# First weight of the first FFN: its loads, conversion and first plain tile, two steps sooner

## The chip, the cores and the metric

One core of a Trainium2 chip runs the whole program. The metric is the device time of one execution in microseconds (us); the median of several executions is compared. PE is TensorE (matmul), DVE is VectorE, ACT is ScalarE, POOL is GpSimd, SP is the engine whose queue issues most of the DMAs here.

## What is computed

A decayed linear attention (retention) over 4 batches, 8 heads, 768 positions and a head size of 64, followed by two feed-forward layers on the 3072 x 512 result.

```python
for t in range(S):
    state = gamma[None, :, None, None] * state + np.einsum('bhd,bhe->bhde', k[:, :, t], v[:, :, t])
    y[:, :, t] = scale * np.einsum('bhd,bhde->bhe', q[:, :, t], state)
...
h = x @ w_in                      # 3072x512 @ 512x2048
g = np.maximum(0.01 * h, h)
x = g @ w_out                     # 3072x2048 @ 2048x512
...
h = x @ w_in                      # the second layer, with its own weights
g = h * (1.0 / (1.0 + np.exp(-1.702 * h)))
y = g @ w_out
```

The weights arrive as 64-bit words (low and high 32-bit halves) and the kernel turns them into 32-bit floats itself.

## The kernel before, in words

**Order of the work.** The program is scheduled by hand: each engine, and SP's queue, executes its instructions in the order in which the Python code emits them. So the order of the calls in the loop of `retention()` (lines 378 to 404) is the order on every engine.

**Retention, 24 steps.** A step `s` is one chunk of 128 positions of one batch (4 batches of 6 chunks, `c` is the chunk's number in its batch), all 8 heads. `a_load(s)` (L263) brings 1 MB of q, k and v into a ring of four places. `a_scores(s)` (L269) makes the scores on PE (L277) and multiplies them by the decay mask on DVE (L280); its PSUM banks 0 and 1 are the only ones for scores, so the scores of the next step wait for that mask product. `a_decay(s)` (L283) scales k on ACT in eight instructions (L288), and is left out in the last chunk of a batch (steps 5, 11, 17, 23). `a_out(s)` (L290) has the matmuls for the state (L300), for scores times v (L307) and for state times q (L313), and the state's scaling on DVE (L316); L300 and L316 are missing in the last chunk of a batch, L313 in the first. `a_store(s, o)` (L320) scales the result out of PSUM: in steps 0 to 7 in three DVE instructions (L332), afterwards in one (L345). In steps 0 to 3, which make the tokens of block 0, ACT then rounds the result to the matmul format (L341) and POOL subtracts to get the remainder (the subtraction of `subtract`, L151): these two parts are the operand `x0`, 128 columns of it per step.

**The loop** prepares step `s + 1`'s scores, runs `a_out(s)`, does the first half of a weight's work (`work_first`, L216), `a_store(s)`, the second half (`work_last`, L222), `a_decay(s + 2)`, `a_load(s + 4)` and last the plain tiles of that step (`ffn_in(0, m)`, L231).

**Weight work.** Weight `m` of 16 is one 128 x 512 slice of the first layer's `w_in`. `load_raw(m)` (L165) loads 512 KB through SP into a ring of three places. `convert(m)` (L193) runs two ACT instructions (L172, L173) and four DVE instructions (L176, L178, L180, L182), from a ring of two places. `work_last(n)` rounds weight `n` up (L191: on POOL for weights 0 and 1, on DVE afterwards) and finishes weight `n - 1`: a rounding cast on ACT (L154) and a subtraction on DVE (L151) give the weight's two parts. `work_first(n)` also loads raw weight `n + 2`, before it converts weight `n`.

**Plain tiles.** `ffn_in(0, m)` multiplies weight `m` with block 0 of the tokens: 12 matmuls of 128 x 512 (L238), three for each quarter of the 512 inputs: weight's high part with the remainder of `x0`, high with high, the weight's remainder with the high part. ACT applies the leaky ReLU (L242) and its queue stores the result (L244).

**When.** The constant `W0` and the list `now_in` set the step of each tile, and the condition in line 385 derives from them the steps of the weight work:

```python
W0 = 6
now_in = [[m for m in range(KF) if W0 + m * (N_STEPS - W0) // KF == s] for s in range(N_STEPS)]
...
if s >= W0 - 2 and done[0] < KF + 1 and (s <= W0 or now_in[s - 1]):
```

Before, weight work begins in step 4, tile 0 is in step 6, tiles 0 to 7 are in steps 6 to 13, tiles 8 to 15 in steps 15 to 22. Raw weights 0 and 1 are loaded at the end of steps 1 and 2, raw weight 2 in step 4.

**Afterwards** the blocks 1 to 5 of the first layer's `x @ w_in` follow (L238 again), then three products in a seven-product form (L776, L583, L776).

Of the kernel before, what the change touches and what calls it, by code (L numbers as in the profile page):

```python
# [87 lines left out]
def retention_two_ffn(ctx: ExitStack, tc: tile.TileContext, qkv, consts, small, w1i, w1o, w2i, w2o, scratch, out):  # L88
# [76 lines left out]
    def load_raw(m):  # L165
        raw[m] = t = next(raw_ring).bitcast(U32)
        nc.sync.dma_start(out=t, in_=w1i[m].bitcast(U32).rearrange("p (f two) -> p f two", two=2))
# [39 lines left out]
    def x_split(q, k):  # L207
        split(xs[q % 2][k][:, 0], xs[q % 2][k][:, 1], x_raw[:, k])
        if k == NP - 1 and q + 1 < NB:
            x_load(q + 1)  # L210

    W0 = 6
    now_in = [[m for m in range(KF) if W0 + m * (N_STEPS - W0) // KF == s] for s in range(N_STEPS)]
    done = [0]

    def work_first(n):  # L216
        if n + 2 < KF:
            load_raw(n + 2)
        if n < KF:
            convert(n)  # L220

    def work_last(n):  # L222
        if n < KF:
            round_up(*conv[n], nc.gpsimd if n < 2 else nc.vector)
        if 0 < n <= KF:
            finish(n - 1)
# [4 lines left out]
    def ffn_in(blk, m, place=None):  # L231
        h = banks[:, h_banks[i_h[0] % len(h_banks)]]
        i_h[0] += 1
        w = wt[m].rearrange("p s (k f) -> p s k f", k=NP)
        i = 0
        for k in range(NP):
            for a, c in ((0, 1), (0, 0), (1, 0)):
                nc.tensor.matmul(out=h, lhsT=w[:, a, k], rhs=xs[blk % 2][k][:, c], start=(i == 0),  # L238
                                 stop=(i == 3 * NP - 1), skip_group_check=True)
                i += 1  # L240
        t = next(g_ring) if place is None else place
        nc.scalar.activation(out=t, in_=h, func=AF.Lrelu)  # L242
        if place is None:
            nc.scalar.dma_start(out=gd1[m][:, blk * TB : blk * TB + TB], in_=t)  # L244

    def retention():
# [16 lines left out]
        def a_load(s):  # L263
            ins[s] = next(in_ring)
            n = 2 if s < 3 else 4
            for i in range(0, 4, n):
                nc.sync.dma_start(out=ins[s][:, i : i + n], in_=qkv[s, :, i : i + n])

        def a_scores(s):  # L269
            t = ins[s]  # L270
            qT = t[:, 0].rearrange("p (n i) -> p n i", n=NP)
            kT = t[:, 1].rearrange("p (n i) -> p n i", n=NP)
            ps = banks[:, 0:2].rearrange("p e (n i) -> p e n i", n=NP)
            for n in range(NP):
                for e in range(2):
                    r = slice(D * e, D * e + D)
                    nc.tensor.matmul(out=ps[:, e, n], lhsT=kT[r, n], rhs=qT[r, n], start=True, stop=True,  # L277
                                     skip_group_check=True)
            sm = next(sm_ring)
            nc.vector.tensor_tensor(out=sm, in0=ps, in1=mask, op=ALU.mult)  # L280
            sc_t[s] = sm

        def a_decay(s):  # L283
            b, c = steps[s]
            if c < NC - 1:
                ks_t[s] = ins[s][:, 2].rearrange("p (h d) -> p h d", h=H)
                for h in range(H):
                    nc.scalar.activation(out=ks_t[s][:, h], in_=ks_t[s][:, h], func=AF.Copy, scale=kdec[:, c, h : h + 1])  # L288

        def a_out(s):  # L290
            b, c = steps[s]
            t = ins.pop(s)
            sm, ks = sc_t.pop(s), ks_t.pop(s, None)
            q = t[:, 0].rearrange("p (n i) -> p n i", n=NP)
            v = t[:, 3].rearrange("p (n f) -> p n f", n=NP)
            if c < NC - 1:
                for n in range(NP):
                    for e in range(2):
                        r = slice(D * e, D * e + D)
                        nc.tensor.matmul(out=kv[r, n], lhsT=ks[:, 2 * n + e], rhs=v[:, n, r],  # L300
                                         start=(c == 0 and n == 0), stop=True, skip_group_check=True)
            o = next(o_ring)
            out = lambda n, e: o[D * (e ^ (n & 1)) : D * (e ^ (n & 1)) + D, n % 2, n // 2 * P : n // 2 * P + P]
            for n in range(NP):
                for e in range(2):
                    r = slice(D * e, D * e + D)
                    nc.tensor.matmul(out=out(n, e), lhsT=v[:, n, r], rhs=sm[:, e, n], start=(n < 2),  # L307
                                     stop=(c == 0), skip_group_check=True)
            if c > 0:
                for n in range(NP):  # L310
                    for e in range(2):
                        r = slice(D * e, D * e + D)
                        nc.tensor.matmul(out=out(n, e), lhsT=st[c % 2][r, n], rhs=q[r, n], start=False, stop=True,  # L313
                                         skip_group_check=True)
            if c < NC - 1:
                nc.vector.tensor_tensor(out=st[(c + 1) % 2], in0=kv, op=ALU.mult,  # L316
                                        in1=gdec[:, c + 1, :].unsqueeze(2).to_broadcast([P, NP, D]))
            return o

        def a_store(s, o):  # L320
            blk, cc = divmod(s, CPB)
            cols = slice(cc * P, cc * P + P)
            if blk == 1:
                x = x_raw[:, :, cols]
            else:
                if cc % 2 == 0:
                    a_store.x = next(x_ring)
                x = a_store.x[:, :, cc % 2 * P : cc % 2 * P + P]

            def put(r, u, t):  # L330
                n = 2 * P
                nc.vector.tensor_tensor(out=x[r].rearrange("p (m u) i -> p u m i", u=2)[:, u],  # L332
                                        in0=o[t, u, :n].rearrange("p (m i) -> p m i", i=P),
                                        in1=qdec[t].rearrange("p (m u) i -> p u m i", u=2)[:, u], op=ALU.mult)

            if blk < 2:
                put(slice(0, P), 0, slice(0, P))
                for r, t in halves:
                    put(r, 1, t)
            if blk == 0:  # L340
                nc.scalar.copy(out=x0[:, :, 0, cols], in_=x)  # L341
                subtract(x0[:, :, 1, cols], x, x0[:, :, 0, cols].bitcast(F32), nc.gpsimd)
            if blk < 2:
                return
            nc.vector.tensor_tensor(out=x.rearrange("p (m u) i -> p u m i", u=2),  # L345
                                    in0=o[:, :, : 2 * P].rearrange("p u (m i) -> p u m i", i=P),
                                    in1=qdec.rearrange("p (m u) i -> p u m i", u=2), op=ALU.mult)
            if cc % 2:
                swapped(xd0[blk][:, :, cc * P - P : cc * P + P], a_store.x)
# [19 lines left out]
        def keep_warm(n):  # L369

            for _ in range(n):
                nc.tensor.matmul(out=warm, lhsT=idle[:, :P], rhs=idle, start=True, stop=True, skip_group_check=True)  # L372
# [5 lines left out]
        for s in range(len(steps)):  # L378
            if s == 0:
                keep_warm(6)  # L380
            elif s + 1 < len(steps):
                a_scores(s + 1)
            o = a_out(s)
            n = None
            if s >= W0 - 2 and done[0] < KF + 1 and (s <= W0 or now_in[s - 1]):
                n = done[0]
                done[0] += 1
                work_first(n)
            if s == 0:
                a_scores(1)  # L390
                keep_warm(6)
            a_store(s, o)
            if n is not None:
                work_last(n)
            if s + 2 < len(steps):
                a_decay(s + 2)
            if s + 4 < len(steps):
                a_load(s + 4)
            if s in (1, 2):
                load_raw(s - 1)  # L400
            if s >= len(steps) - 4:
                x_split(1, s - len(steps) + 4)
            for m in now_in[s]:
                ffn_in(0, m)
# [454 lines left out]


    retention()

    h_banks[:] = range(6)
# [252 lines left out]
```

## Time and profile before

| | |
|---|---|
| median of 3 runs | 1050.0 us (1049.67 to 1050.69) |
| the profiled execution's own time | 1051.16 us |
| its span, first to last instruction | 1049.4 us |
| PE busy | 1040.3 us, 99% of the span |
| DVE busy | 821.4 us, 78% |
| ACT busy | 576.4 us, 55% |
| POOL busy | 72.3 us, 7% |
| mean DMA rate | 213 GB/s |

PE's busy time is modelled from pipelined instructions, so a busy PE is not PE at its peak; the idle time of PE is what to look for. Rows of a timeline have the start in us from the span's start, the duration, engine, line, operation, what is written and read, and how many instructions are merged; in square brackets the idle time of that engine before the row, and what ended it. Instructions on DVE and ACT overlap a little, so the distance of two starts is often shorter than the first one's duration.

### The profile page before, as it was taken

To read this page: it belongs to the slowest core of one execution; us is meant where nothing else is said; L and a number is where in the kernel's file an instruction comes from. 1 tells how busy PE (TensorE), PEld (TensorE's weight loads), DVE (VectorE), ACT (ScalarE), POOL (GpSimd) and SP (SyncE) were. 2 spreads that over 40 slices of the span, in tenths; PEclk is the share of its full clock that TensorE was granted. 3 is DMA by queue.
4 is the path that set the end of the run, shared out by engine and by line. 5 is a ranking of instruction groups with operands and counts; after the bars stand their busy time and mean duration, and the time that the engine had idled before them with its cause. 6 is when DMAs were issued, how large, how long until landed. Compare 5 with 4: busy or idle time off the path is not lost.

```text
span 1049.4 us, 16867 instructions
## 1 busy us (share of the span) xinstructions
PE 1040.3 (99%) x5955; PEld 892.8 (85%) x5955; DVE 821.4 (78%) x1417; ACT 576.4 (55%) x1103; POOL 72.3 (7%) x75
## 2 busy tenths in 40 slices
PE   9999999999999999999999999999999999999998
PEld 6778788888888888888888999999999878888886
DVE  5988739876885798787788677686868898887986
ACT  5776446554555654544546566564657644545443
POOL 2100000000000000000000104434410000000000
PEclk9999999999999999999999999999999999999999
DMA  8989677999896423524439846747477725635624
GB/s 323 366 321 352 227 231 234 314 320 317 312 339 223 151 81 131 190 80 163 158 85 327 305 162 205 238 163 290 158 274 253 266 81 134 188 90 138 174 81 80
DMA packets 167557, 223.72 MB, mean 213 GB/s; under 512 B 57264, under 2 KB 112304, under 8 KB 164272
## 3 DMA queue, kind: packets, MB, share of 16 engines
q1 hardware_dynamic: 132608, 175.67, 51.6%
q10 hardware_dynamic: 34864, 46.97, 12.2%
q8 instruction: 46, 0.75, 0.3%
q14 instruction: 39, 0.32, 0.1%
HBM read 137.66 MB, written 84.93 MB: 212 GB/s over the span
## 4 chain that ended last, share of the span: by engine, by line
PE 93%; DVE 4%; DMA 1%; issue 1%; ACT 0%; ACTq 0%; SPq 0%; DVEq 0%
PE psum L776 39%; PE psum L238 25%; PE psum L583 22%; PE psum L277 2%; PE psum L307 2%; PE psum L300 1%; PE psum L313 1%; DVE e L151 1%; DVE c L784 0%; DMA d<-gd 0%; DMA h<-qkv 0%; PE psum L372 0%; ACTq L1004 0%; DVE c L996 0%; DVE a L741 0%
## 5 line engine op out<-in xcount | busy, mean ns | idle before, releaser
L776 PE MATMUL psum<-c,h 128*128 128x512 f32 x1008 | 228.8, 389 | 0.0
L776 PEld LDWEIGHTS psum<-c,h 128*128 128x128 f32 x1008 | 189.2, 188 | 39.3
L776 PE MATMUL psum<-e,h 128*128 128x512 f32 x768 | 179.8, 389 | 0.9 <-DVE e L151 0.9
L776 PEld LDWEIGHTS psum<-e,h 128*128 128x128 f32 x768 | 144.0, 188 | 31.6 <-DVE e L151 0.9
L238 PE MATMUL psum<-d,h 128*128 128x512 f32 x576 | 136.2, 393 | 0.5 <-DVE h L151 0.5
L238 PE MATMUL psum<-a,h 128*128 128x512 f32 x576 | 131.2, 389 | 0.0
L238 PEld LDWEIGHTS psum<-d,h 128*128 128x128 f32 x576 | 106.8, 188 | 25.6 <-issue 2.1
L238 PEld LDWEIGHTS psum<-a,h 128*128 128x128 f32 x576 | 108.0, 188 | 22.6 <-issue 0.2
L583 PE MATMUL psum<-c,h 128*128 128x384 f32 x576 | 110.1, 334 | 0.3 <-DVE d L620 0.3
L583 PE MATMUL psum<-b,h 128*128 128x384 f32 x576 | 110.1, 334 | 0.0
L583 PEld LDWEIGHTS psum<-c,h 128*128 128x128 f32 x576 | 100.7, 188 | 0.7 <-DVE d L620 0.6
L583 PEld LDWEIGHTS psum<-b,h 128*128 128x128 f32 x576 | 100.6, 188 | 0.3 <-ACT psum L656 0.2
L729 ACT CAST c<-b 128x512 fp32r<-128x512 f32 x96 | 59.3, 622 | 57.4 <-DVE c L151 35.6
L603 ACT ACTIVATE d<-psum 128x384 f32<-128x384 f32 x96 | 47.1, 492 | 62.8 <-PE psum L583 54.8
L151 DVE TENSOR_TENSOR c<-b,c 128x512 fp32r<-128x512 f32 x96 | 65.4, 690 | 18.8 <-ACT c L729 16.6
L242 ACT ACTIVATE e<-psum 128x512 f32<-128x512 f32 x80 | 47.5, 593 | 54.8 <-PE psum L238 52.4
L729 ACT CAST e<-a 128x512 fp32r<-128x512 f32 x77 | 47.7, 622 | 47.2 <-PE psum L776 22.2
L151 DVE TENSOR_TENSOR h<-h 128x384 fp32r<-128x384 f32 (+2 forms) x80 | 43.9, 584 | 27.8 <-ACT h L154 19.6
L151 DVE TENSOR_TENSOR e<-a,e 128x512 fp32r<-128x512 f32 x77 | 52.4, 686 | 9.5 <-ACT e L729 8.6
L607 DVE TENSOR_TENSOR d<-psum,d 128x384 f32<-128x384 f32 x96 | 52.1, 550 | 5.0 <-ACT d L603 2.6
L151 POOL TENSOR_TENSOR a<-a 128x768 f32<-128x768 f32 x7 | 13.3, 1894 | 586.4 <-PE psum L776 540.8
L776 PE MATMUL psum<-f,h 128*128 128x512 f32 x192 | 48.7, 389 | 0.0
(147 smaller groups left out, 1428.8 us busy)
## 6 DMA issues: line engine op xcount, KB each, us to landing
gd<-d ACTq DMA_DIRECT2D x128, 192.0 KB, 3.5
h<-qkv SPq DMA_DIRECT2D x21, 1024.0 KB, 7.9
gd<-e ACTq DMA_DIRECT2D x80, 256.0 KB, 5.0
d<-gd SPq DMA_DIRECT2D x64, 256.0 KB, 3.8
b<-gd SPq DMA_DIRECT2D x64, 256.0 KB, 3.9
a<-gd SPq DMA_DIRECT2D x48, 256.0 KB, 4.7
c<-w1i SPq DMA_DIRECT2D x16, 512.0 KB, 7.7
xd<-e SPq DMA_DIRECT2D x12, 512.0 KB, 3.1
```

Source lines behind the costliest of these rows:

```text
L151: e.tensor_tensor(out=o, in0=x, in1=y, op=ALU.subtract)
L238: nc.tensor.matmul(out=h, lhsT=w[:, a, k], rhs=xs[blk % 2][k][:, c], start=(i == 0), stop=(i == 3 * NP - 1), skip_group_check=True)
L242: nc.scalar.activation(out=t, in_=h, func=AF.Lrelu)
L277: nc.tensor.matmul(out=ps[:, e, n], lhsT=kT[r, n], rhs=qT[r, n], start=True, stop=True, skip_group_check=True)
L300: nc.tensor.matmul(out=kv[r, n], lhsT=ks[:, 2 * n + e], rhs=v[:, n, r], start=(c == 0 and n == 0), stop=True, skip_group_check=True)
L307: nc.tensor.matmul(out=out(n, e), lhsT=v[:, n, r], rhs=sm[:, e, n], start=(n < 2), stop=(c == 0), skip_group_check=True)
L313: nc.tensor.matmul(out=out(n, e), lhsT=st[c % 2][r, n], rhs=q[r, n], start=False, stop=True, skip_group_check=True)
L583: nc.tensor.matmul(out=t, lhsT=w[:, k, a], rhs=x[:, b, k], start=(start and m == 0), stop=(m == 5), skip_group_check=True)
L603: nc.scalar.activation(out=s, in_=src, func=AF.Sigmoid, scale=1.702)
L607: nc.vector.tensor_tensor(out=dst, in0=src, in1=s, op=ALU.mult)
L729: nc.scalar.copy(out=t[:, 0], in_=self.block_of(*item))
L776: nc.tensor.matmul(out=t[:, j], lhsT=w[:, j, a], rhs=x[:, b], start=(new and q == 0 and m == 0), stop=(q == NQ - 1 and m == 2), skip_group ...
```

## The change

`W0` becomes 4. From that follow: weight work begins in step 2, tile 0 is in step 4, tiles 0 to 3 are in steps 4 to 7, tiles 4 to 7 in 9 to 12, tiles 8 to 11 in 14 to 17, tiles 12 to 15 in 19 to 22. Steps 8, 13 and 18 have weight work and no tile; steps 9, 14 and 19 have a tile and no weight work. The first two raw loads stand in steps 0 and 1 and ahead of `a_load(s + 4)` instead of behind it in steps 1 and 2; raw weight 2 is loaded in step 2.

```diff
-    W0 = 6
+    W0 = 4
     now_in = [[m for m in range(KF) if W0 + m * (N_STEPS - W0) // KF == s] for s in range(N_STEPS)]
     done = [0]
...
             if s + 2 < len(steps):
                 a_decay(s + 2)
+            if s in (0, 1):
+                load_raw(s)
             if s + 4 < len(steps):
                 a_load(s + 4)
-            if s in (1, 2):
-                load_raw(s - 1)
             if s >= len(steps) - 4:
                 x_split(1, s - len(steps) + 4)
             for m in now_in[s]:
```

## Rows read from the trace of the kernel before

**Rows 1.** The page, chain of work that ended last, by engine.
```profile
PE 93%; DVE 4%; DMA 1%; issue 1%; ACT 0%; ACTq 0%; SPq 0%; DVEq 0%
```

**Rows 2.** Waits of PE, first 132.6 us: who waited for whom, total us, times, longest.
```profile
PE psum L277 <- DMA h<-qkv: 1.2, 2, 0.7
...
PE psum L277 <- DVE b L280: 1.0, 1, 1.0
PE psum L238 <- DVE h L151: 0.5, 1, 0.5
```

**Rows 3.** Waits of PE after 132.6 us, the longest of three.
```profile
PE psum L776 <- DVE e L151: 0.9, 2, 0.5
```

**Rows 4.** Timeline of PE, first 60 us: the score matmuls of steps.
```profile
5.36 2.08 PE L277 MATMUL psum<-h 64*128 64x128 f32 x16 [0.51 <-DMA h<-qkv]
...
20.55 1.16 PE L277 MATMUL psum<-h 64*128 64x128 f32 x16
...
23.73 1.16 PE L277 MATMUL psum<-h 64*128 64x128 f32 x16
...
31.47 1.16 PE L277 MATMUL psum<-h 64*128 64x128 f32 x16 [0.97 <-DVE b L280]
...
37.80 1.16 PE L277 MATMUL psum<-h 64*128 64x128 f32 x16
...
43.95 1.16 PE L277 MATMUL psum<-h 64*128 64x128 f32 x16
```

**Rows 5.** Chain in order of time, first 60 us: start, us, what.
```profile
21.71 0.61 PE psum L300 x16
...
23.20 0.60 PE psum L313 x16
```

**Rows 6.** Timeline of DVE, 12 to 60 us.
```profile
18.80 1.23 DVE L280 TENSOR_TENSOR b<-psum,b 128x1024 f32<-128x1024 f32 x1
19.94 0.41 DVE L316 TENSOR_TENSOR b<-psum,f 128x256 f32<-128x256 f32 x1
...
26.63 0.79 DVE L176 TENSOR_SCALAR c<-c 128x512 uint32<-128x512 uint32 x1
...
31.33 0.42 DVE L176 TENSOR_SCALAR c<-c 128x512 uint32<-128x512 uint32 x1
...
33.19 1.29 DVE L332 TENSOR_TENSOR c<-psum,f 128x256 f32<-128x256 f32 x3
34.51 0.74 DVE L151 TENSOR_TENSOR h<-b,h 128x512 fp32r<-128x512 f32 x1
35.17 1.21 DVE L280 TENSOR_TENSOR b<-psum,b 128x1024 f32<-128x1024 f32 x1
...
41.01 1.22 DVE L280 TENSOR_TENSOR b<-psum,b 128x1024 f32<-128x1024 f32 x1
```

**Rows 7.** Timeline of ACT, 12 to 60 us.
```profile
19.33 2.02 ACT L288 ACTIVATE h<-h,f 128x64 f32<-128x64 f32 x8
21.98 0.62 ACT L341 CAST d<-h 128x512 fp32r<-128x512 f32 x1 [0.64 <-DVE h L332]
22.51 2.02 ACT L288 ACTIVATE h<-h,f 128x64 f32<-128x64 f32 x8
...
27.66 2.02 ACT L288 ACTIVATE h<-h,f 128x64 f32<-128x64 f32 x8 [0.71 <-DMA h<-qkv]
29.59 0.66 ACT L172 ACTIVATE b<-c 128x512 f32<-128x512 f32 x1
```

**Rows 8.** Timeline of POOL, first 160 us.
```profile
25.86 1.28 POOL L151 TENSOR_TENSOR d<-h,d 128x512 fp32r<-128x512 f32 x1 [1.91 <-ACT d L341]
29.09 1.30 POOL L191 TENSOR_TENSOR b<-b,c 128x512 int32<-128x512 int32 x1 [1.95 <-ACT h L288]
```

**Rows 9.** Stretches: PE, PEld, DVE, ACT, POOL busy us, PE clock, DMA share, GB/s.
```profile
16.00:18.00 2.00, 2.00 (x42) 1.66 (x40) 1.47 (x4) 1.94 (x9) 1.27 (x1) 1.00 0.40 160
```

**Rows 10.** DMA issues, the loads of q, k and v: times, KB each, us to landing.
```profile
h<-qkv SPq DMA_DIRECT2D x21, 1024.0 KB, 7.9
```

## The prediction

> **What bounds the kernel now.** I read first the chain that ended last: 93% of it is PE [rows 1], so the time is PE's work plus PE's waits, and a wait that is added or removed anywhere on PE shows in full at the end unless a later wait shrinks by it. Then the waits of PE, split at 132.6 us, where retention ends. Afterwards the longest entry is 0.9 us in two waits [rows 3]: hardly anything there can absorb a delay. Within retention the waits that the change can reach are three: 0.7 for an input, 1.0 for the mask product, 0.5 for the remainder of weight 0 [rows 2]; the other 0.5 of the DMA entry is the wait before the first scores [rows 4]. So the change can gain some 2.7 us at most, and lose whatever new waits it makes. Last the timelines of PE, DVE and ACT around the steps 1 to 8.
>
> **PE's own arithmetic.** A step without a tile takes 23.73 - 20.55 = 3.18 us, a step with one 43.95 - 37.80 = 6.15 [rows 4]; a tile is 2.97. All 24 steps and 16 tiles stay, so PE's work stays, and only waits count. From 23.73 to 37.80 the kernel before runs steps 4, 5 and 6 and tile 0 in 14.07 us; the work in them is 3 x 3.18, less L300 in step 5 and L313 in step 6 (0.6 each [rows 5]; 0.5 of the first, since neighbours overlap), plus 2.97, some 11.4. The three places cost 14.07 - 11.4 = **2.65 us**; from step 7 on PE is not held up.
>
> **The change part by part.** The weight work of steps 4 and 5 moves into steps 2 and 3. There ACT and DVE do something that steps 4 and up don't: the cast of L341, which waits for L332, with `a_decay(s + 2)` behind it on ACT. Both engines go in order, so a weight converted in step `s` waits on ACT for the decay of step `s - 1`, that for its cast, and that for its L332, while on DVE the L332 of step `s` now stands behind the conversion. That is a ring, and it can be walked with durations from the rows.
>
> *Step 2.* The decay of step 1 starts at 19.33 [rows 7]. What follows it on ACT starts 29.59 - 27.66 = 1.93 later, so L172 of weight 0 runs from 21.26 to 21.92. DVE is done with L316 at 20.35 [rows 6] and idles until 21.95. From L176 to L332 is 33.19 - 31.33 = 1.86, so L332 starts at 23.81. The next mask product starts as long after L332 as L151 does in 34.51 - 33.19 = 1.32: at 25.13, and ends 1.23 later at 26.36. Step 5's scores, at 23.73 before, can't start until 26.4: **wait 2.7**.
>
> *Step 3.* L341 starts when L332 is done, 25.13; decay 4 starts 22.51 - 21.98 = 0.53 later [rows 7], L172 of weight 1 another 1.93 later, 27.59 to 28.25. L176 at 28.28, L332 at 30.14 to 31.43, L341 at 31.46. Decay 4 also holds L300 of step 4, to 27.7: **0.2**. The cast of weight 0 follows L341 and ends near 32.6. POOL's subtraction, the last quarter of `x0`, starts 0.70 after L341 and takes 1.28 [rows 8]: done at 33.45. Tile 0 starts with the remainder of `x0`, so it starts at 33.5. PE was through with step 4 at 26.4 + 0.2 + 3.18 = 29.8: **wait 3.7**. Here the two steps sooner meet the last of `x0`, which before had long been there.
>
> *Steps 4 to 9.* DVE now runs 41.01 - 35.17 = 5.84 per step with a tile [rows 6], PE 6.15, so PE only slowly gets room. L151 of weight 0 at 32.63 and 0.66 [rows 6] for the next start give a mask product at 33.3; steps of 5.84 (5.4 in step 5, which has no L316) put weight 1's remainder at 39.2, as PE wants it at 36.5 + 2.7: **0 to 0.3**. The mask product of step 9 comes near 56.3 to 57.3 and ends 1.23 later. Before, no tile is missing until step 14; now step 8 has none, so PE, at 53.9 with step 9's scores, wants the next scores 3.18 later, 57.1 to 57.3: **0.5 to 1.2**. After it step 9 has no weight work, DVE catches up, and steps 13 and 18 find it ahead, as step 14 did before: nothing.
>
> *One rule against it.* L176 took 0.79 instead of 0.42 [rows 6] while POOL subtracted from 25.86 to 27.14 [rows 8]: it ended 0.28 after POOL did. L151 of weight 0 would now start at 32.6 within POOL's subtraction (32.2 to 33.45), and I take it as held, so that the mask product comes at 33.95. The Trainium skill, State Buffer, "Who interferes with whom", says that a DVE instruction with two SBUF inputs contends with a GpSimd instruction that reads SBUF, and the later one blocks. With it the last two terms are at their upper ends, without it at their lower; row 26.63 agrees for another kind of DVE instruction.
>
> *DMAs and queues.* Raw 0 now goes into SP's queue at once behind `a_load(3)`, ahead of `a_load(4)`, and raw 1 ahead of `a_load(5)`. That puts 0.5 MB each before inputs; the DMA engines are only 0.40 busy from 16 to 18 us [rows 9], so input 4 is in by then with room for it. Bounds: nothing lost, and up to the 0.7 that PE waits for an input now [rows 2] gained, since input 6 is wanted later (36.5 instead of 23.73 + 3.18 = 26.9); lost, at most another 0.7, if input 4 came that late. I take 0 beyond the walk, in which the 0.7 is gone already. Raw 3 waits on SP for POOL's L191 of weight 0, which now queues behind the subtraction of step 2 (25.83 + 1.28 + 1.30 [rows 8] = 28.4), and `a_load(7)` behind it; with 7.9 to landing [rows 10] that input is there at 36.5, wanted at 42. Cover enough. L191 of weight 0 is off POOL before the subtraction at 32.2. The store of each tile moves along on ACT's queue and stays 16 times.
>
> **Sum.** New waits 2.7 + 0.2 + 3.7 + (0 to 0.3) + (0.5 to 1.2) = 7.1 to 8.1; taken away 2.65: 4.5 to 5.5 us slower. Since row 26.63 shows the hold, I take 5.2. The profiled execution had 1051.16 and would have 1056.4; it stood 1.16 above the median, so the median goes from 1050.0 to **1055.2 us**.
>
> **The rivals.** *PE's clock falls, 1058.5.* The walk leaves PE without work for 2.7 us and then 3.7, with 3.4 of work between; before, no gap was over 1.0. At its start PE ran the 16 score matmuls in 2.08 instead of 1.16 [rows 4], that is at half pace, so both levels, 1.2 and 2.4 GHz, occur, though the granted clock in the rows is 1.00 [rows 9]. If tile 0 and step 5's small matmuls ran at the lower level they would cost 2.97 + 2.7 again, of which the waits at tile 1 and in step 9 take up to 1.5 and a part would run fast: some 3.3 on top. Against it: PE works between the gaps. The Trainium skill, TensorE: Matmul & The Clock Gate, "Why this matters for your kernels", warns of PE gaps over some 3 us; whether this one reaches that no row shows. Chance 0.12.
>
> *The ring is looser than walked, 1052.5.* If DVE and ACT interleaved so that only tile 0 has to wait for `x0`, the 2.7 would drop out: 5.2 - 2.7. Against: rows 7 show each decay right behind its cast. Chance 0.08.
>
> *Faster, 1047.5.* The three present waits vanish, since conversion lies in steps that PE has without tiles and tile 0 fills step 4: 1050.0 - 2.65. It decides at L172 of weight 0: if that ran before 20.35, where DVE ends L316, L332 of step 2 would start near 22.2, 1.6 sooner, and so on round the ring. It stands behind the decay that starts at 19.33, so it would need the decay to be elsewhere. Even then DVE has 1.14 + 0.41 + 1.86 + 1.32 = 4.7 us of work [rows 6] in a step of 3.18. Chance 0.06.
>
> *Nothing in the end, 1050.* The pile-up of conversion is only moved two steps, its waits cost the same 2.65, and `x0` comes in time. Chance 0.06.
>
> **How the numbers follow.** The forecast gets 0.68. Less than 0.2% (2.1 us) can't be told from no change here: 1047.9 to 1052.1. Faster holds the one rival, 0.06; same the other and an edge of the looser ring, 0.07; slower the rest, 0.87. The range goes from the looser ring to the clock case, 1052.5 to 1058.5; outside lie 0.12 of the two rivals below and edges of the others.
>
> **What would show it.** In the changed timeline: L172 of weight 0 near 21.3, DVE idle before it for 1.6; step 5's scores near 26.4, waiting for L280; tile 0 near 33.5, waiting for POOL's L151; a wait of about 1 before the scores of step 10; retention's end near 138 instead of 132.6. Wrong would be: tile 0 before 32, or L332 of step 2 ahead of the conversion; a tile 0 lasting over 4 us would be the clock.

## The result, and the profile after

The changed kernel takes 1056.19 us (median of 6 runs, 1054.72 to 1057.97) against 1049.67 for the kernel before: a ratio of 1.006, 95% interval 1.0049 to 1.0071, or **6.5 us slower**. The profiled execution took 1056.53 us with a span of 1054.8.

The chain that ended last, by engine, is PE's as before [rows 1], with more of DMA and ACT in it:

```profile
PE 94%; DVE 2%; DMA 2%; ACT 1%; issue 0%; SPq 0%; POOL 0%; DVEq 0%; ACTq 0%
```

The waits of PE in the first 140 us (who waited for whom, total us, times, longest), which answer to [rows 2]:

```profile
PE psum L238 <- POOL d L151: 3.8, 1, 3.8
PE psum L277 <- DMA h<-qkv: 2.3, 4, 0.8
...
PE psum L277 <- DVE b L280: 1.1, 1, 1.1
```

The timeline of PE, which answers to [rows 4]: the scores (L277) of steps 2, 3, 4 and 5, tile 0 (L238), the scores of steps 6, 10 and 21, and the first matmuls behind retention.

```profile
12.62 1.16 PE L277 MATMUL psum<-h 64*128 64x128 f32 x16 [0.39 <-DMA h<-qkv]
...
16.39 1.16 PE L277 MATMUL psum<-h 64*128 64x128 f32 x16 [0.52 <-DMA h<-qkv]
...
20.46 1.16 PE L277 MATMUL psum<-h 64*128 64x128 f32 x16 [0.82 <-DMA h<-qkv]
...
24.82 1.16 PE L277 MATMUL psum<-h 64*128 64x128 f32 x16 [1.11 <-DVE b L280]
...
31.89 5.43 PE L238 MATMUL psum<-d,h 128*128 128x512 f32 x12 [3.83 <-POOL d L151]
37.26 1.16 PE L277 MATMUL psum<-h 64*128 64x128 f32 x16
...
57.78 1.16 PE L277 MATMUL psum<-h 64*128 64x128 f32 x16
...
118.02 1.16 PE L277 MATMUL psum<-h 64*128 64x128 f32 x16 [0.54 <-DMA h<-qkv]
...
138.09 4.15 PE L238 MATMUL psum<-a,h 128*128 128x512 f32 x17
```

What to see: PE is late by four small waits, three for inputs and one of 1.11 us for DVE, and then by a large one, until POOL has the last remainder of `x0`; and tile 0, 12 matmuls that took 3.02 to 3.04 us in each of tiles 1 to 15 before, takes 5.43. The stretches of the same kernel (length in us; PE, PEld, DVE, ACT, POOL busy us, PE clock, DMA share, GB/s) say why:

```profile
28.00:30.00 2.00, 0.07 (x4) 0.00 (x0) 1.82 (x4) 0.12 (x1) 0.00 (x0) 1.00 1.01 389
30.00:31.00 1.00, 0.00 (x0) 0.00 (x0) 0.00 (x0) 1.00 (x2) 0.42 (x1) 0.66 0.98 360
...
32.00:36.00 4.00, 4.00 (x10) 3.14 (x11) 3.93 (x8) 3.58 (x11) 1.56 (x1) 0.50 0.37 131
36.00:38.00 2.00, 2.00 (x16) 1.31 (x16) 1.94 (x5) 0.74 (x2) 0.00 (x0) 0.72 0.99 393
38.00:42.00 4.00, 4.00 (x49) 3.19 (x47) 3.71 (x8) 3.56 (x11) 0.00 (x0) 1.00 0.99 299
```

After 28.1 PE has no work, and its granted clock falls from 1.00 to 0.50, that is from 2.4 to 1.2 GHz; by the means of 0.66 and 0.72 it fell near 30.3 and came back near 37.1, when PE had been at work again since 31.9. The ring itself, on DVE and then on ACT and POOL, which answer to [rows 6], [rows 7] and [rows 8]:

```profile
20.35 0.43 DVE L176 TENSOR_SCALAR c<-c 128x512 uint32<-128x512 uint32 x1 [1.21 <-ACT b L172]
...
22.22 1.28 DVE L332 TENSOR_TENSOR h<-psum,f 128x256 f32<-128x256 f32 x3
23.54 1.23 DVE L280 TENSOR_TENSOR b<-psum,b 128x1024 f32<-128x1024 f32 x1
...
26.70 0.43 DVE L176 TENSOR_SCALAR c<-c 128x512 uint32<-128x512 uint32 x1 [1.60 <-ACT b L172]
...
28.56 1.29 DVE L332 TENSOR_TENSOR h<-psum,f 128x256 f32<-128x256 f32 x3
31.05 1.34 DVE L151 TENSOR_TENSOR h<-b,h 128x512 fp32r<-128x512 f32 x1 [1.20 <-ACT h L154]
```

```profile
17.76 2.01 ACT L288 ACTIVATE h<-h,f 128x64 f32<-128x64 f32 x8
19.68 0.64 ACT L172 ACTIVATE b<-c 128x512 f32<-128x512 f32 x1
...
23.54 0.62 ACT L341 CAST d<-h 128x512 fp32r<-128x512 f32 x1 [2.62 <-DVE h L332]
24.07 2.02 ACT L288 ACTIVATE h<-h,f 128x64 f32<-128x64 f32 x8
25.99 0.67 ACT L172 ACTIVATE b<-c 128x512 f32<-128x512 f32 x1
```

```profile
30.58 1.26 POOL L151 TENSOR_TENSOR d<-h,d 128x512 fp32r<-128x512 f32 x1 [3.82 <-ACT d L341]
31.80 1.76 POOL L191 TENSOR_TENSOR b<-b,c 128x512 int32<-128x512 int32 x1
```

L172 of weight 0 starts right behind the decay, DVE idles for it, L332 stands behind the conversion, L341 behind L332 (ACT idle 2.62 us), the next decay behind L341, and so on once more.

**Where the time goes.** The two profiled executions start differently: the scores of step 2 run at 14.19 us in the one before and at 12.62 here, since PE's matmuls left their half pace sooner (the first six idle matmuls of step 0 take 2.74 us before and 1.47 here). So I compare from there to the end of retention, 132.64 before and 138.09 here. Timeline of PE in the kernel before:

```profile
14.19 1.16 PE L277 MATMUL psum<-h 64*128 64x128 f32 x16
...
132.64 9.59 PE L238 MATMUL psum<-a,h 128*128 128x512 f32 x41
```

I take three stretches: from the scores of step 2 to those of step 5; to those of step 6, with tile 0; to the end. PE's own work is 3 x 3.18 = 9.54 in the first and 6.15 in the second. In the third it is 100.1: the 94.84 that the kernel before takes from 37.80 to 132.64, and 5.25 for steps 5 and 6 without their tiles. Together that is 115.8. The kernel before took 118.45, with its 2.65 us of waits. The changed one took 12.20 + 12.44 + 100.83 = 125.47, **7.0 us more**: 2.66 in the first stretch, 6.29 in the second (3.9 of waiting and 2.4 of slow clock), 0.7 in the third, less the 2.65.

### The profile page after: what moved, and what is told of

Read it like the earlier page. It is cut to its first block, busy times and chain, and to the rows that moved or that the text cites. A ratio compares the mean times of both kernels' runs of the same rounds, so it can differ in the third digit from the quotient of the medians.

```text
span 1054.8 us, 16866 instructions
## 1 busy us (share of the span) xinstructions
PE 1041.1 (99%) x5955; PEld 894.1 (85%) x5955; DVE 823.6 (78%) x1417; ACT 576.8 (55%) x1103; POOL 72.7 (7%) x75
## 3 DMA queue, kind: packets, MB, share of 16 engines
q10 hardware_dynamic: 34864, 46.97, 12.2%
## 4 chain that ended last, share of the span: by engine, by line
PE 94%; DVE 2%; DMA 2%; ACT 1%; issue 0%; SPq 0%; POOL 0%; DVEq 0%; ACTq 0%
PE psum L776 42%; PE psum L238 25%; PE psum L583 22%; PE psum L277 2%; PE psum L307 2%; DMA h<-qkv 1%; PE psum L313 1%; PE psum L300 1%; DVE e L151 0%; ACT h L288 0%; DVE b L741 0%; DVE h L151 0%; DVE a L741 0%; DVE h L332 0%; DMA d<-gd 0%
## 5 line engine op out<-in xcount | busy, mean ns | idle before, releaser
L238 PE MATMUL psum<-d,h 128*128 128x512 f32 x576 | 138.3, 398 | 3.8 <-POOL d L151 3.8
L238 PEld LDWEIGHTS psum<-d,h 128*128 128x128 f32 x576 | 108.5, 191 | 29.1 <-POOL d L151 4.1
L238 PE MATMUL psum<-a,h 128*128 128x512 f32 x576 | 131.2, 389 | 0.0
L238 PEld LDWEIGHTS psum<-a,h 128*128 128x128 f32 x576 | 108.0, 188 | 22.6 <-issue 0.2
L151 DVE TENSOR_TENSOR c<-b,c 128x512 fp32r<-128x512 f32 x96 | 65.4, 690 | 18.8 <-ACT c L729 16.6
L151 DVE TENSOR_TENSOR h<-h 128x384 fp32r<-128x384 f32 (+2 forms) x80 | 43.3, 577 | 28.8 <-ACT h L154 20.2
L151 DVE TENSOR_TENSOR e<-a,e 128x512 fp32r<-128x512 f32 x77 | 52.4, 686 | 9.5 <-ACT e L729 8.6
L151 POOL TENSOR_TENSOR a<-a 128x768 f32<-128x768 f32 x7 | 13.3, 1895 | 593.9 <-DMA h<-wds 547.4
```

What stands on the lines that cost most here:

```text
L151: e.tensor_tensor(out=o, in0=x, in1=y, op=ALU.subtract)
```

## The experiments

Each was timed beside the kernel before, and the differences are against its median there: 1050.02 us for the loads alone, one step sooner with the new loads, the idle matmuls and the tiles one step later; 1049.97 for the loads behind the inputs with W0 = 4, ACT's two instructions first, both of these together, and finishing a weight first; 1050.18 for the two kernels without the loads; 1049.85 for the loads alone behind the inputs and one step sooner with the old loads.

### The loads alone

```diff
 W0 = 6
...
+            if s in (0, 1):
+                load_raw(s)
             if s + 4 < len(steps):
                 a_load(s + 4)
-            if s in (1, 2):
-                load_raw(s - 1)
```

> The kernel before with one part of the change: raw weights 0 and 1 are loaded in steps 0 and 1 ahead of the inputs, W0 stays 6. Theory (the ring of L332, L341, decay and L172, then the clock): the loads cost nothing; the 0.7 us that PE waits for input 6 goes, but the next scores wait for the mask product of DVE, which ends at 31.4 as before, so the time stays: -0.3 to +0.5 us against the kernel before. Rival 1 (the loads delay inputs 2 to 5; the changed kernel has PE waits of 0.39, 0.52 and 0.82 us for them): +1 to +2 us. Rival 2 (the DMA wait was a real cost before): -0.7 us.

1052.94 us, ratio 1.0026 (1.0016 to 1.0035): +2.9. The theory falls here. Rival 1 has the cause, late inputs, and was too low, though its upper end of +2 lies within the interval. Timeline of PE, the scores of steps 3 and 4, and a stretch (columns as above):

```profile
16.11 1.16 PE L277 MATMUL psum<-h 64*128 64x128 f32 x16 [0.49 <-DMA h<-qkv]
...
21.10 1.23 PE L277 MATMUL psum<-h 64*128 64x128 f32 x16 [1.74 <-DMA h<-qkv]
```

```profile
22.00:24.00 2.00, 2.00 (x29) 1.81 (x28) 1.56 (x2) 1.26 (x6) 0.69 (x1) 0.52 1.03 430
```

Input 4 is late by 1.74 us, and the clock falls behind that wait, so that step 4's matmuls, too, run at half pace. Over the nine executions the time goes with the clock: 1050.27 to 1052.45 us where its mean is 0.999 or 1.00, 1052.94 to 1054.41 where it is 0.997 or 0.998. So much of the 2.9 goes with the clock.

### The loads alone, behind the inputs

```diff
 W0 = 6
...
             if s + 4 < len(steps):
                 a_load(s + 4)
-            if s in (1, 2):
-                load_raw(s - 1)
+            if s in (0, 1):
+                load_raw(s)
```

> The kernel before (W0 = 6) with raw weights 0 and 1 loaded in steps 0 and 1, one step sooner, but still behind the input of that step. Theory (the 2.9 us of the loads alone come from raw 0 standing ahead of input 4 in the queue, which is wanted first): input 4 is on time, 0 to +1 us against the kernel before. Rival (the bytes count wherever they stand, input 5 is then as late as input 4 was): +2 to +3 us.

1050.61 us, ratio 1.0006 (0.9997 to 1.0015): +0.8, not told from no change, as the theory has it. Six waits for inputs, none over 0.6 us, and the clock at 1.00. So with W0 = 6 it is the place ahead of input 4 that costs, not the bytes.

### One step sooner, with the new loads and with the old ones

```diff
-    W0 = 4
+    W0 = 5
```

> The changed kernel with W0 = 5: weight work begins in step 3, tile 0 is in step 5. Theory: the ring is gone through once, not twice: L172 of weight 0 waits for the decay that begins at 22.5 (24.4), L332 of step 3 starts near 27.0 instead of 23.8, step 6's scores wait some 2.7 us, tile 0 about 1.0 for its weight's remainder, which replace 2.65: +1.0 us against the kernel before (+0.5 to +1.8), and with no PE gap over 3 us the granted clock stays at 1.00. Rival (the cost goes with the number of steps): half of what the change costs, +3.2 us. Rival (only tile 0 meeting the last quarter of x0 costs): no difference, since x0 is done before step 5's tile.

1053.02 us, ratio 1.0029 (1.0018 to 1.004): +3.0. The theory falls, and the rival that halves the cost of the change (+3.2) is near. Timeline of PE, the last ten matmuls of tile 0:

```profile
34.38 3.81 PE L238 MATMUL psum<-d,h 128*128 128x512 f32 x10 [2.05 <-DVE h L151]
```

The wait for the weight's remainder is 2.05 us where about 1.0 was expected, and behind it the clock falls, which was not expected: its mean is 0.60 from 35 to 37 us, and the ten matmuls take 3.81 where they took 2.57 before. Is it the loads or the step that costs? The same one step with the loads where they were:

```diff
-    W0 = 6
+    W0 = 5
```

> The kernel before with W0 = 5 and the loads where they were (raw 0 and 1 at the end of steps 1 and 2, behind the inputs). Weight work begins in step 3, tile 0 is in step 5. Theory (the 3.0 us of W0 = 5 with the new loads are mostly the loads, the ring gone through once costs little): 0 to +1.5 us against the kernel before. Rival (the weight work costs 1.5 us for each step that it is sooner, whatever the loads): +2.5 to +3.5 us, with tile 0 again waiting over 1.5 us for DVE.

1053.32 us, ratio 1.0034 (1.0022 to 1.0047): +3.5. The theory's size falls and the rival's holds, though PE waits before the scores of step 6 and not at tile 0 (0.73 us). Timeline of PE (scores of step 6) and of DVE:

```profile
28.41 2.08 PE L277 MATMUL psum<-h 64*128 64x128 f32 x16 [2.60 <-DVE b L280]
```

```profile
29.31 1.51 DVE L178 TENSOR_SCALAR b<-b 128x512 f32<-128x512 f32 x1
```

Once round the ring is 2.60 us, the 2.7 of the walk. What the walk left out stands beside it: those scores take 2.08 instead of 1.16, the clock having fallen in the gap (mean 0.54 from 28 to 30 us), and L178 takes 1.51 instead of 0.41 beside POOL's L191 (29.06 to 30.53).

### No loads of raw 0 and 1

```diff
-            if s in (0, 1):
-                load_raw(s)
...
+        for m in range(2):
+            raw[m] = next(raw_ring).bitcast(U32)
+            nc.gpsimd.memset(raw[m].bitcast(F32), 0.0)
         keep_warm(8)
```

> The changed kernel without the loads of raw weights 0 and 1: POOL sets their two places to zero at the start instead, so 1 MB less goes through the DMA queue and nothing stands ahead of the inputs (the tiles 0 and 1 are multiplied with zeros). All the rest is the change. Theory (the ring alone makes most of the loss, the loads' waits lie inside it): +4.5 to +6.5 us against the kernel before; no PE wait for inputs 3 to 5 over 0.5, the wait before step 5's scores 2.5 or more, tile 0 after a wait of 1 to 4, the clock falling in one of them. Rival (ring and loads add up): 6.5 - 2.9 = +3.6 us or less.

1056.33 us, ratio 1.0056 (1.0044 to 1.0068): +6.15, as the theory has it and not told from the change's 6.5. Timeline of PE, the scores of steps 3 and 5 and tile 0:

```profile
16.16 1.16 PE L277 MATMUL psum<-h 64*128 64x128 f32 x16 [0.52 <-DMA h<-qkv]
...
24.61 1.16 PE L277 MATMUL psum<-h 64*128 64x128 f32 x16 [1.60 <-DVE b L280]
...
31.70 4.69 PE L238 MATMUL psum<-d,h 128*128 128x512 f32 x12 [3.84 <-POOL d L151]
```

The wait for DVE is only 1.60 where 2.5 was expected, because inputs 3 and 4 are late here as well, by 0.52 and 0.35 us. But from the scores of step 2, at 12.39, to those of step 5 it takes 12.22 us, with the loads 12.20: the same sum, 2.7 over PE's work. What the inputs hold up, the ring needs anyway. So the 2.9 us that the loads cost alone are not to be found in the change.

### The loads behind the inputs, with W0 = 4

```diff
-            if s in (0, 1):
-                load_raw(s)
             if s + 4 < len(steps):
                 a_load(s + 4)
+            if s in (0, 1):
+                load_raw(s)
```

> The changed kernel with raw weights 0 and 1 loaded in the same steps 0 and 1, but behind the input instead of ahead of it (two lines change places). The loads alone cost +2.9 us with W0 = 6. Theory (with W0 = 4 the ring hides most of what the loads cost, since the scores of step 5 and tile 0 wait for it in any case): the PE waits for inputs 2, 3 and 4 (0.39, 0.52, 0.82) go, the wait for DVE before step 5's scores grows instead; 0.5 to 1.5 us less than the change: +5 to +6 us against the kernel before. Rival (the two costs add): the 2.9 us go in full: +3.5 us. Rival (the position in the queue does not matter, only the number of bytes): +6.5 us.

1057.14 us, ratio 1.0066 (1.0054 to 1.0079): +7.2; the theory's gain did not come. Of the rivals, the one by which the place in the queue does not matter (+6.5) is the nearest. Timeline of ACT and of PE:

```profile
20.76 0.69 ACT L172 ACTIVATE b<-c 128x512 f32<-128x512 f32 x1 [0.88 <-DMA c<-w1i]
```

```profile
25.94 2.08 PE L277 MATMUL psum<-h 64*128 64x128 f32 x16 [3.04 <-DVE b L280]
```

Behind input 4, raw 0 is late for its conversion by 0.88 us and the ring starts later by that. The PE wait is now in one piece of 3.04 us, and the clock falls there (mean 0.50 from 26 to 30 us) instead of at tile 0.

### ACT's two instructions ahead of the decay

```diff
+            if s in (1, 2):
+                convert_scalar(s - 1)
             if s + 2 < len(steps):
                 a_decay(s + 2)
```

`convert_scalar(m)` emits L172 and L173 of weight `m`; `convert(m)` then has the four DVE instructions alone.

> The changed kernel with the two ACT instructions (L172, L173) of weights 0 and 1 emitted one place earlier, at the end of steps 1 and 2 ahead of the decay, so that the first of them no longer stands behind that decay. Theory (the ring): L332 of steps 2 and 3 start 1.2 and 2.9 us sooner than in the changed kernel (21.0 and 25.7 instead of 22.2 and 28.6), tile 0's wait for POOL's subtraction falls from 3.8 to about 1 us and the clock does not fall there; later DVE sets the pace and the mask product of step 9 takes back 1.5 to 2: +2.5 to +4 us against the kernel before. Rival (the ring is not what delays tile 0, DVE's amount of work is): tile 0 starts within 0.5 us of where it does in the changed kernel, +6 to +7 us.

1053.88 us, ratio 1.0036 (1.0024 to 1.0048): +3.9, within the theory's range and 2.6 us less than the change. The ring is a cause, shown by cutting it, of a part of the loss. Timeline of PE (lines are 10 higher here: the scores of step 4, tile 0, the scores of step 21) and of DVE:

```profile
20.45 1.16 PE L287 MATMUL psum<-h 64*128 64x128 f32 x16 [1.21 <-DMA h<-qkv]
...
30.22 4.69 PE L248 MATMUL psum<-d,h 128*128 128x512 f32 x12 [2.60 <-POOL d L151]
...
116.56 1.16 PE L287 MATMUL psum<-h 64*128 64x128 f32 x16 [1.59 <-DMA h<-qkv]
```

```profile
24.26 1.51 DVE L178 TENSOR_SCALAR b<-b 128x512 f32<-128x512 f32 x1
```

L332 of step 3 starts at 26.90 instead of 28.56, not at 25.7: L176 (0.79) and L178 (1.51) stand beside POOL's L151 and L191. Tile 0 still waits 2.6 us, where about 1 was expected, and the clock still falls (mean 0.50 from 32 to 34 us). This profiled execution, 1057.37 us, is the slowest of its six.

The loads behind the inputs and ACT's two instructions first, both together:

> The two edits together: the ACT instructions of weights 0 and 1 ahead of the decay, and the loads of raw 0 and 1 behind the inputs. Theory (ring and loads are two costs, and both are now mostly out): +1 to +3 us against the kernel before; what is left is DVE's amount of work ahead of tile 0. Rival (raw 0 lands too late for an ACT instruction that now stands ahead of decay 3, and holds up that decay): +3 to +5 us, with PE waiting for L288.

1056.32 us, ratio 1.006 (1.0047 to 1.0072): +6.35. What the rival names is seen, but the time is worse than its +3 to +5. Waits of PE (L310 are the state's matmuls, L298 the decay, both 10 lines higher than in the change):

```profile
PE psum L310 <- ACT h L298: 1.5, 1, 1.5
```

L172 waits 3.19 us for raw 0 and, being ahead of decay 3 now, holds it and PE behind it. So the early conversion gains only with the loads ahead of the inputs: +3.9 there, +6.35 here.

### Idle matmuls ahead of tile 0

```diff
+            if s == W0:
+                keep_warm(12)
             for m in now_in[s]:
```

> The changed kernel with 12 idle matmuls (128x512, bf16, into the bank that tile 0 then overwrites) in step 4 ahead of tile 0, where PE waits 3.8 us. They add 2.8 us of PE work at full pace inside the wait. Theory (the fallen clock is a part of the loss of its own): tile 0 takes 3.0 instead of 5.4 us, the granted clock stays at 1.00; of the 2.4 us the mask product of step 9 takes back 0.5 to 1.2: 1.2 to 2.4 us less than the changed kernel's 6.5, so +4.1 to +5.3 us against the kernel before. Rival (the half clock only covers waits that DVE sets anyway): +6.5 us as without them.

1055.64 us, ratio 1.0053 (1.0041 to 1.0065): +5.6, between the theory and the rival. The intervals of this and of the change overlap, so the time alone does not settle it; the trace of one execution says more. Timeline of PE: tile 0, then the scores of steps 6, 10, 15 and 21:

```profile
31.64 3.11 PE L238 MATMUL psum<-d,h 128*128 128x512 f32 x12 [0.63 <-POOL d L151]
34.68 1.16 PE L277 MATMUL psum<-h 64*128 64x128 f32 x16
...
56.40 1.16 PE L277 MATMUL psum<-h 64*128 64x128 f32 x16 [0.92 <-DVE b L280]
...
84.27 1.16 PE L277 MATMUL psum<-h 64*128 64x128 f32 x16 [1.12 <-DMA h<-qkv]
...
118.13 1.16 PE L277 MATMUL psum<-h 64*128 64x128 f32 x16 [0.98 <-DMA h<-qkv]
```

The clock stays at 1.00, tile 0 takes 3.11, and from the scores of step 5 (25.06) to those of step 6 PE takes 9.62 us instead of 12.44. Then it is given back: 0.92 for the mask product of step 9, and 1.12 and 0.98 for inputs 15 and 21, which come soon behind steps without a tile. From the scores of step 6 to the end of retention, at 138.17, it takes 103.49 us instead of 100.83. So the fallen clock is real, but of the 2.8 us that it costs at tile 0 the later waits take back 2.7 in this execution.

### The tiles one step later

```diff
-            for m in now_in[s]:
+            for m in now_in[s - 1] if s else ():
```

> The changed kernel with every plain tile of block 0 one step later (tile 0 in step 5 instead of 4, the last one in step 23), weight work and loads as in the change. Theory (the ring on ACT and DVE sets the time, tile 0 only stands where the wait comes out): step 6's scores then wait for the mask product of step 5, which ends near 33.5 in the changed kernel, so PE idles 5.5 us instead of 3.8 and the tile is still to do: 1 to 3 us worse than the change, +7 to +9.5 us against the kernel before, and the clock falls as well. Rival (tile 0 meeting the last quarter of x0 is the loss): the 3.8 us wait and the fall of the clock go, +0 to +2.5 us against the kernel before.

1057.98 us, ratio 1.0073 (1.006 to 1.0086): +8.0, as the ring has it; the rival falls. Timeline of PE, the scores of step 6:

```profile
33.56 2.08 PE L277 MATMUL psum<-h 64*128 64x128 f32 x16 [5.50 <-DVE b L280]
```

Without tile 0 in step 4 PE waits 5.50 us instead of 3.83. That tile 0 met the last quarter of `x0` names the releaser, not the cause.

### No loads, the ring cut, and six idle matmuls

The edits of three runs above, with `keep_warm(6)`; tiles 0 and 1 are multiplied with zeros again.

> As the run before it (no loads of raw 0 and 1, zeros instead), and also the ACT instructions of weights 0 and 1 ahead of the decay, and 6 idle matmuls in step 4 ahead of tile 0. Theory (with loads, ring and clock out, what is left is DVE's amount of work ahead of tile 0 and the inputs that come late behind a step without a tile): +0.5 to +2.5 us against the kernel before, the granted clock at 1.00 throughout. Rival (DVE's amount of work alone makes the loss, ring or not): +3.5 us or more.

1054.49 us, ratio 1.0043 (1.0029 to 1.0056): +4.3, on the rival's side (+3.5 or more) and not the theory's. Timeline of PE: tile 0, the scores of steps 10 and 21:

```profile
30.31 3.11 PE L248 MATMUL psum<-d,h 128*128 128x512 f32 x12 [1.22 <-POOL d L151]
...
55.09 1.16 PE L287 MATMUL psum<-h 64*128 64x128 f32 x16 [0.92 <-DVE b L290]
...
115.97 1.16 PE L287 MATMUL psum<-h 64*128 64x128 f32 x16 [1.11 <-DMA h<-qkv]
```

The clock is at 1.00, and from step 2 on no wait of PE in retention is over 1.22 us; ahead of tile 0 the idle matmuls fill another 1.2. Even so, from step 2's scores to the end of retention it takes 123.51 us (12.51 to 136.02), 5.1 more than before. DVE is busy without a gap from 17.46 to 28.27, and the last instruction of that stretch, L332 of step 3 (L342 here), starts the cast and POOL's subtraction for which tile 0 waits. So what remains is DVE, by its amount of work beside the four steps that also make `x0`, and by POOL's hold on it: L176 of weight 1 takes 0.80 us, L178 1.51 and L151 of weight 0 1.34, where they take 0.42, 0.42 and 0.68 elsewhere. That is 2.1 us, which I take as an estimate of the most that POOL's part can be.

### Finishing a weight first, in the kernel before

```diff
+        if 0 < n <= KF:
+            finish(n - 1)
         if n < KF:
             convert(n)
...
-        if 0 < n <= KF:
-            finish(n - 1)
```

> The kernel before (W0 = 6, loads as before) with the finish of weight n - 1 (cast L154, subtraction L151) moved from the end of a step's weight work to its start, ahead of the conversion of weight n. Nothing else moves. Theory (in the kernel before the first tiles wait for a DVE that is behind by its order of work): the 0.5 us wait of tile 0 goes and PE need not wait for a weight's remainder any more, but the scores of steps 7 and 9 still wait for the mask products: -0.3 to -1.5 us against the kernel before. Rival (DVE's amount of work sets it): 0. Rival (the cast on ACT ahead of the conversion delays the conversion, and the finish on DVE delays L332): +0.5 to +1 us.

1049.99 us, ratio 0.9997 (0.9988 to 1.0005): no difference, so the theory falls and the first rival holds. Timeline of PE, the scores of step 7 and tile 0:

```profile
30.23 1.16 PE L277 MATMUL psum<-h 64*128 64x128 f32 x16 [1.26 <-DVE b L280]
...
32.81 3.02 PE L238 MATMUL psum<-d,h 128*128 128x512 f32 x12
```

Tile 0's wait is gone, the wait before it is longer (1.26 instead of 0.97): that fits DVE's amount of work there too. None of the twelve is faster than the kernel before.

## Why the prediction was right, and where it was not

*The bound* held: PE is 94% of the chain, and what its waits add in retention comes out at the end, since the waits behind 138 us are those of before, the longest again 0.9.

*The signs.* Counted from the scores of step 2, the walk is met to 0.1 us: L172 of weight 0 at 7.07 in the walk (21.26 - 14.19) and 7.06 measured (19.68 - 12.62), step 5's scores at 12.2 and 12.20, tile 0 at 19.3 and 19.27. In the trace's own times tile 0 starts at 31.89, before the 32 that I had set as a sign of being wrong; that is the start of this execution, 1.57 us earlier, which a sign in absolute times does not allow for. The end of retention, expected near 138 and found at 138.09, is luck for the same reason: counted from step 2 it is 125.47 against 123.8, so 1.7 later than walked. The wait of about 1 before the scores of step 10 is missing, and tile 0 lasts over 4 us, the sign of the clock.

*Step 2, wait 2.7.* The ring is there link by link: L172 starts 1.92 us behind its decay (1.93 in the walk), the mask product 1.32 behind L332. The sum is 2.66 in the first stretch, 2.60 where it stands alone (one step sooner, old loads). In the changed kernel it is spread over three scores, two of them waiting for inputs.

*Step 3, wait 3.7.* Measured 3.83, and 3.84 without the loads. The 0.2 for the state's matmul did not show. The tiles one step later show that the ring, not `x0`, sets the moment.

*The hold on DVE.* L151 of weight 0 took 1.34 us, beginning within POOL's subtraction (30.58 to 31.84) and ending 0.55 after it, so the row 26.63 had been read rightly. The rule of the Trainium skill (SBUF — State Buffer, "Who interferes with whom"), that a DVE instruction with two SBUF inputs contends with a GpSimd instruction that reads SBUF, agrees with it. I applied the hold once; when the order moved it came again on an instruction with one tensor input: L178 took 1.51 us in five of the runs.

*Tile 1 and step 9's mask product.* Nothing at tile 1. The wait before the scores of step 10 (0.5 to 1.2) is not in the changed kernel, because PE came later by the slow clock; where tile 0 ran at full pace it is 0.92, in two runs shown above.

*The clock.* This is the term that was wrong: I put it at nothing and made it a rival with a chance of 0.12. The mean granted clock was 0.996 to 0.998 in all six runs of the changed kernel, against 0.998 to 1.00 in 15 runs of the kernel before. It cost 2.4 us at tile 0, took the place of the 0.5 to 1.2, and so moved the sum from 5.2 to some 6.6 (an estimate, 5.2 - 1.0 + 2.4); the run with the idle matmuls, 0.9 us below the change and not told from it, puts the net effect lower than these 1.4. Of the rival's two terms only tile 0 came: the scores behind it take 1.16 again. So two misses, the clock and the wait that it covered, cancel in part, and that the forecast is only 1.3 us short of the 6.5 is luck to that extent. By its own size the walk had 7.1 to 8.1 of new waits; measured are 2.66 + 3.9 + 2.4 + 0.7 = 9.7 in the profiled execution. The forecast of 1055.2 and the clock case of 1058.5 have the measured 1056.19 between them.

*The DMAs at 0.* Right in the sum, wrong in its reason. I held that input 4 would be in by then with room for it; it was 0.82 us late, and with W0 = 6 the same two lines cost 2.9 us. The row that I read, a share of 0.40 from 16 to 18 us, is the slackest of its neighbours: before, the share is 1.00 from 14 to 16 us and 0.97 from 20 to 22, and in the changed kernel it is 0.99 to 1.05 all the way from 12 to 24. The loads cost next to nothing here (6.15 without them, 6.5 with them) because the ring is waited for in any case. The 0.54 for an input behind step 18, which has no tile, was not foreseen.

*The other rivals.* The looser ring and the faster case needed L172 to come sooner; with that forced, the time is still +3.9, and the combined run puts that down to DVE, which is full there. That nothing changes in the end is out: the loss is 6.5 us, by the interval 5.1 to 7.5. Left open is how the remaining 4.3 us of the combined run divide between DVE's work and POOL's hold on it, which by the rows is at most some 2.1: no run took POOL's part away.

## What to carry to other kernels

Before work is moved forward into a stretch that shows idle slots, walk the in-order queues link by link through that stretch: an instruction that waits on one engine and has another engine's input behind it closes a ring, and the ring's period, not the sum of work, is then the step's time. Where one of the engines is full besides, as DVE is here, cutting the ring gives back only a part (2.6 of 6.5 us). Two costs measured apart need not add: here the 2.9 us that the loads cost alone lay, as far as can be told, inside a wait that the ring made. A new gap on PE is priced with the clock that it may take along (it fell behind gaps of 2.05 to 5.50 us in seven of the kernels here, and not behind one of 2.30 in another), and a repair of the clock with the waits that it uncovers.

## What was not expected of the hardware

The granted clock fell in gaps shorter than those of which the prediction quotes a warning, and the measurement decides. It fell while PE waited 3.83 us in the changed kernel and 3.04 in another, but also in waits of 2.60 us in two more, behind a wait of 2.05 (one step sooner, new loads), behind a wait of 1.74 that followed one of 0.49 (mean 0.52 from 22 to 24 us), and, with the loads behind the inputs and ACT's two instructions first, behind a wait of 1.52 and 15 matmuls that were kept waiting one by one (1.92 us; mean 0.50 from 26 to 28). It did not fall where PE waited at most 1.26 at a time, as in the kernel with the finish first, nor behind a wait of 1.88 for input 4 in the kernel with the idle matmuls, nor behind one of 2.30 before tile 0 with the loads behind the inputs and ACT's two instructions first (the tile took 3.11); so a wait of that size can go either way. Once fallen, it stayed for 6.8 us in the changed kernel (30.3 to 37.1), with PE at work in 5.2 of them.

POOL and DVE held each other both ways: DVE's L151 took 1.34 instead of 0.68 and L178 1.51 instead of 0.42, while POOL's L191, beginning at 31.80 while that L151 ran, took 1.76 instead of 1.30 [rows 8].
